# A Fourier mixing and ReGLU kernel: order of loads, products and tables in its set-up

## The chip, the cores and the metric

The kernel runs on one core of one Trainium2 chip. Its time is the device time of one execution in microseconds (us), smaller is better. An engine here is one of PE (TensorE, matrix products; PEld is its weight load), DVE (VectorE), ACT (ScalarE), POOL (GpSimd) and SP (SyncE, which here only issues transfers). Each engine works through its own list of instructions in order, and waits on semaphores for what others make. Transfers are issued from SP, ACT and POOL and run on 16 shared DMA engines.

## The reference

The input x has 8 batches of 3008 rows of 256 channels in float32. Each batch goes through a Fourier transform over its rows and one over its channels, of which the real part is kept; then follows a gated feed-forward layer with 1536 hidden units.

```python
X = np.fft.fft(x, axis=1)
X = np.fft.fft(X, axis=2)
y = X.real.astype(np.float32).reshape(8 * 3008, 256)
gate = np.maximum(y @ w_gate, 0.0)
val = y @ w_val
out = (gate * val @ w_out).astype(np.float32)
```

## The kernel before

The real part of the two transforms is U·C − V·S in effect: U and V are transforms of x over its rows with cosines and with sines, and the transform over the channels is folded into the weights. TA and TB (128 x 2 x 128, bf16) are the cosine and sine tables over the channels; WA = TA·w and WB = TB·w are the folded weights, for gate (index 0) and value (index 1). The row transform uses the symmetry of cosine and sine: a row and its mirror row are added first (XD holds rows of x, XG holds the mirror rows, AA their sums; F and G are what goes into the products), and tables tabC and tabS hold cosine and sine for six groups of 128 rows (c = 0 to 5). Row groups are handled in three tiles, t = 0, 1, 2, each with two halves r = 0, 1 (and a parity). Each half of a tile of XD or XG holds 256 KB.

All batches but the first are prepared while the matmuls of an earlier batch run. The first one can't be: before the main loop can start, the kernel has to load batch 0, make all tables and the folded weights, and do a first part of the row transform (the function dft_first, from L605). This is the set-up, the first 18.6 us of the profile. The order of work on each engine is written out by hand there; no scheduler moves it. After it the PE runs two products and a mirrored one for each of 12 blocks of hidden units (first_tile), with the second half of the folded weights (weights, L419, products L427) between them, and from the ninth block on also the output products (L782), which need the matrix wo.

The steps of the set-up that the change and the prediction touch:

- Loads of batch 0. The upper mirror rows of tile 0 (XG, L126) and rows of tile 0 (XD, L113) go out on SP and ACT, then rows of tile 1 on SP (L96). The rows of tile 2 are loaded by `load_rows(0, (2,))` (L96) with `load_last(0)` (L102) behind it; these stand on SP and wait for two writes to the same tile: `hold` (L116), a one-element memset on POOL whose only use is that the load has to wait for it, and a memset of the last 32 partitions on DVE (L381).
- Mirror rows of tiles 1 and 2: four indirect gathers on POOL (L120, load_mirror), (t, r) = (1,0), (1,1), (2,0), (2,1), called M10, M11, M20, M21 below. Between them stand small iota instructions (L274) that fill urow, from which the PE makes the angles; urow has one pair of rows for each pair of c.
- Behind the gathers POOL loads the weights (L342): first the 512 columns that dft_first needs (called w00 for gate, w10 for value), later four more such blocks, and wo (L417).
- turn(r) (L395) on PE puts the mirror rows of half r of tile 0 in the right order, by a float32 product with a reversed identity matrix. angle(n, c) makes the tables of one c: two products on PE (L360, L361), then three steps on ACT (L364 sine, L365 absolute value, L366 cosine). spin(n) issues n products on zeros (L326).
- On DVE, for each tile: sums AA (L472 and L473 for a half of tile 0, L461 and L462 for tiles 1 and 2), F (L441, L439), the middle channel hy (L447), G (L455). ACT then makes the small vector ny from hy (whole_128, L451).
- In dft_first: products(t, 0, ..) multiply F with tabC and products(t, 1, ..) multiply G with tabS (both L622); nyquist(t) multiplies ny with tabC (L628); combine(i) makes the first 512 columns of WA and WB (L636), gate first.
- The second halves of TA and TB are the first halves with signs changed on odd columns (L655, L656 on ACT). Column 0 of both is written by POOL (L349, L409).

Before the change the order on PE is: turn(0), the angles of c = 3, turn(1), the angles of c = 2, then in dft_first the products of tile 0 with the angles of c = 5 and 4 between them, tile 1, combine(0), tile 2, combine(1).

Of the kernel before, what the change touches and what calls it, by code (L numbers as in the profile page):

```python
# [15 lines left out]
ALU = mybir.AluOpType  # L16
# [13 lines left out]
def dram(ap, offset, pattern):  # L30
    return bass.AP(ap.tensor, offset, [list(p) for p in pattern])
# [3 lines left out]
def kernel(  # L35
# [8 lines left out]
    nc = tc.nc  # L44
    B, S, D = x.shape
    DF = moe_w_gate.shape[1]
    NF = DF // 128
    H = S // 2
# [14 lines left out]
    def single(name, shape, dt=F32, pool=const):  # L63
        return pool.tile(shape, dt, name=name, tag=name)
# [3 lines left out]
    WA = [single(f"WA{i}", [128, DF], BF16) for i in range(2)]  # L68
# [9 lines left out]
    XD = single("XD", [128, 2, 3, 2, D])  # L78
# [14 lines left out]
    def load_rows(b, ts=range(3)):  # L93
        for t in ts:
            n = (128, 128, 112)[t]
            nc.sync.dma_start(out=XD[0:n, :, t].rearrange("p r a d -> p r (a d)"),  # L96
                              in_=dram(x, (b * S + 1 + t * 256) * D, [[2 * D, n], [H * D, 2], [1, 2 * D]]))

    def load_last(b):
        for a in range(2):  # L100
            n = (8, 7)[a]
            nc.sync.dma_start(out=XD[112:112 + n, :, 2, a, :], in_=dram(x, (b * S + 1 + 2 * (256 + 112) + a) * D, [[2 * D, n], [H * D, 2], [1, D]]))  # L102
# [12 lines left out]
    def hold(ts):  # L115
        nc.gpsimd.memset(XD[0:1, :, ts, 0, 0:1], 0.0)  # L116

    def load_mirror(b, t, r):
        n = (128, 128, 120)[t]
        nc.gpsimd.indirect_dma_start(  # L120
            out=XG[0:n, r, t, :, :].rearrange("p a d -> p (a d)"), out_offset=None, in_=pairs,
            in_offset=bass.IndirectOffsetOnAxis(ap=gidx[0:n, 2 * t + r:2 * t + r + 1], axis=0), element_offset=b * S * D)
# [144 lines left out]
    for r in range(2):  # L267
        load_half(0, r, (nc.sync, nc.scalar)[r])
    load_rows(0, (1,))
    load_mirror_0(0)  # L270
    load_spare()

    def iota(dst, pattern, base, mult):
        nc.gpsimd.iota(dst, pattern=pattern, base=base, channel_multiplier=mult, allow_small_or_imprecise_dtypes=True)  # L274
# [21 lines left out]
    def scale(N):  # L296
        return 2.0 * PI / N * (1.0 - 1e-6)

    KA, UC, KC = 95, 256.0, 128.0
    urow = single("urow", [KA, 6, 128], F16, pool=st_)  # L300
# [6 lines left out]
    TA = single("TA", [128, 2, 128], BF16)  # L307
    TB = single("TB", [128, 2, 128], BF16)
    md = single("md", [128, 129], pool=st_)
    ad = single("ad", [128, 129], pool=st_)  # L310
# [11 lines left out]
    def spin(n):  # L322
        if n:
            p = psO.tile([128, 512], F32, name="o", tag="o")
        for _ in range(n):
            nc.tensor.matmul(p[:], lhsT=warm[:, 0:128], rhs=warm[:], start=True, stop=True)  # L326
# [7 lines left out]
    iota(back[:], [[0, 1]], 127, -1)  # L334
    iota(gidx[:].rearrange("p (t r) -> p t r", r=2), [[-128, 3], [-H // 2, 2]], H - 1, -1)
    load_mirror(0, 1, 0)
    iota(urow[0:1, 2:4], [[1, 2], [2, 128]], 257, 0)
    load_mirror(0, 1, 1)
    hold(slice(2, 3))

    def load_w(i, c):
        nc.gpsimd.dma_start(out=wr[i][c], in_=(moe_w_gate, moe_w_val)[i][:, c * 512:(c + 1) * 512].rearrange("(c p) f -> p c f", p=128))  # L342
    for r in range(2):
        load_mirror(0, 2, r)
    iota(urow[0:1, 4:6], [[1, 2], [2, 128]], 513, 0)
    nc.gpsimd.memset(urow[0:1, 5, 120:121], 0.0)
    load_w(0, 0)
    load_w(1, 0)
    nc.gpsimd.memset(TA[:, 0, 0:1], 0.5)  # L349

    nc.vector.tensor_scalar(us[:], u[:], scalar1=1.0 / S, op0=ALU.mult, scalar2=None)
    nc.scalar.activation(ums[:], half_pi[:], ACTF.Sin)
# [4 lines left out]
    def angle(n, c):  # L357
        home, tag = ((psG, "g"), (psD, "d"))[n % 2]
        m = home.tile([128, 512], F32, name=tag, tag=tag)
        nc.tensor.matmul(m[:, 0:NJ], lhsT=urow[:, c, :], rhs=krow[:], start=True, stop=False)  # L360
        nc.tensor.matmul(m[:, 0:NJ], lhsT=minus[:], rhs=quot[c][:], start=False, stop=True)  # L361
        r = slice(0, ROWS[c % 2][c // 2])
        act = nc.scalar.activation
        steps = [lambda: act(tabS[r, c, odd_k], m[r, 0:NJ], ACTF.Sin, scale=scale(S)),  # L364
                 lambda: act(mag[c][:], m[:, 0:NJ], ACTF.Abs),  # L365
                 lambda: act(tabC[r, c, odd_k], mag[c][r], ACTF.Sin, scale=-scale(S), bias=half_pi[r])]  # L366
        for step in steps if c != 4 else steps[1:] + steps[:1]:
            step()
# [10 lines left out]
    quotient(5)  # L379
    quotient(4)  # L380
    nc.vector.memset(XD[96:128, :, 2, 1, :], 0.0)  # L381
    load_rows(0, (2,))
    load_last(0)
    nc.vector.tensor_scalar(ums[:], pidx[:], scalar1=1.0 / D, op0=ALU.mult, scalar2=None)
    nc.vector.tensor_scalar(qd[:], dvec[:], scalar1=ums[:], op0=ALU.mult, scalar2=ROUND, op1=ALU.add)
# [7 lines left out]
    def turn(r):  # L393
        p = psV.tile([128, 512], F32, name="v", tag="v")
        nc.tensor.matmul(p[:], lhsT=turned[:], rhs=XG[:, r, 0, :, :].rearrange("p a d -> p (a d)"), start=True, stop=True)  # L395
        upright.append(p[:].rearrange("p (a d) -> p a d", a=2))

    spin(3)
    angle(0, 1)
    angle(1, 0)  # L400
    turn(0)
    nc.scalar.activation(ad[:], md[:], ACTF.Abs)
    nc.scalar.activation(TA[:, 0, 1:128], ad[:, 1:128], ACTF.Sin, scale=-scale(D), bias=half_pi[:])
    nc.scalar.activation(TB[:, 0, 1:128], md[:, 1:128], ACTF.Sin, scale=-scale(D))
    angle(2, 3)
    turn(1)
    angle(3, 2)

    nc.gpsimd.tensor_scalar(TB[:, 0, 0:1], ad[:, 128:129], scalar1=-1.0 / 128, op0=ALU.mult, scalar2=0.5, op1=ALU.add)  # L409
    iota(kvec[:, 0:NE], [[2, NE]], 0, 0)  # L410
    nc.gpsimd.memset(sg[:], 2.0)
    for i in range(2):
# [36 lines left out]
    def whole_128(t):  # L449
        p = slice(0, ROWS[1][t])  # L450
        nc.scalar.mul(ny[p, t], hy[p, t], 2.0)  # L451
# [5 lines left out]
    for t in range(3):  # L457
        n = ROWS[1][t]
        p = slice(0, n)
# [153 lines left out]
    def dft_first(U, V):  # L613

        raw, ends = [], [family(0, dst, 1, False, now=False, pool=pool) for dst, pool in ((U, (psP, "p")), (V, (psO, "o")))]
        bank = {(k, par): ends[k][2](par) for k in range(2) for par in (1, 0)}

        def products(t, k, rs):
            src, tab = ((FF[1], tabC), (GG[1], tabS))[k]
            for r, par in [(r, par) for r in rs for par in (1, 0)]:  # L620
                rows = slice(0, ROWS[par][t])
                nc.tensor.matmul(bank[k, par][:, 0:NJ], lhsT=src[rows, r, t, par, 0:128], rhs=tab[rows, 2 * t + par, odd_k],  # L622
                                 start=(t == 0 and r == 0), stop=(t == 2 and r == 1), skip_group_check=bool(k))

        def nyquist(t):
            for par in (1, 0):
                rows = slice(0, ROWS[par][t])
                nc.tensor.matmul(bank[1, par][0:1, 0:NJ], lhsT=ny[rows, t, par:par + 1], rhs=tabC[rows, 2 * t + par, odd_k],  # L628
                                 start=False, stop=False, skip_group_check=True)

        def combine(i, js):
            for j in js:
                home, tag = ((psV, "v"), (psV, "v"), (psG, "g"), (psD, "d"))[len(raw)]
                p = home.tile([128, 512], F32, name=tag, tag=tag)
                for kc in range(2):
                    nc.tensor.matmul(p[:], lhsT=(TA, TB)[j][:, kc, :], rhs=wr[i][0][:, kc, :], start=(kc == 0), stop=(kc == 1))  # L636
                raw.append(p)

        def whole(W, p):
            return W[:, 0:512], p[:]  # L640

        def by_vector(W, p):
            nc.vector.tensor_scalar(*whole(W, p), scalar1=1.0, op0=ALU.mult, scalar2=None)

        products(0, 0, (0,))
        products(0, 1, (0,))
        whole_128(0)
        angle(4, 5)
        products(0, 0, (1,))
        products(0, 1, (1,))  # L650
        nyquist(0)
        angle(5, 4)
        whole_128(1)
        for T in (TA, TB):
            nc.scalar.copy(T[:, 1, 0::2], T[:, 0, 0::2])  # L655
            nc.scalar.mul(T[:, 1, 1::2], T[:, 0, 1::2], -1.0)  # L656
        products(1, 0, (0, 1))
        nyquist(1)
        products(1, 1, (0, 1))
        combine(0, (0, 1))  # L660
        whole_128(2)
        nc.scalar.copy(*whole(WA[0], raw[0]))
        products(2, 0, (0, 1))
        ends[0][1](1)
        ends[0][1](0)
        evict.pop(0)()
        nc.vector.tensor_scalar(m2[:], pidx[:], scalar1=1.0, op0=ALU.min, scalar2=-2.0, op1=ALU.mult)
        sums[0]()
        by_vector(WB[0], raw[1])
        nyquist(2)  # L670
        products(2, 1, (0, 1))
        ends[1][1](1)
        ends[1][1](0)
        evict.pop(0)()
        sums[2]()
        combine(1, (0, 1))
        nc.scalar.copy(*whole(WA[1], raw[2]))
        nc.scalar.copy(*whole(WB[1], raw[3]))  # L678
        for k in (1, 3):
            sums[k]()  # L680
        del sums[:]
# [138 lines left out]
    EVEN_AT = (8, 10, 12, 14, 16, 17)  # L820
    CB = U
    dft_first(U, V)
    fold_even()
    turns_and_rows()
# [458 lines left out]
```

## Time and profile before

| what | us |
|---|---|
| median of 3 runs | 628.52 |
| lowest and highest run | 628.43, 628.83 |
| the profiled execution, its own time | 628.41 |
| its span from first to last instruction | 626.4 |
| busy PE / DVE / POOL / ACT | 618.8 / 547.7 / 523.4 / 455.6 |
| idle time of PE in the span | 7.6 |

In rows of the profile a line has start and duration in us, the engine, the source line (L), the operation, the tile it writes and those it reads, and in square brackets the idle time before it with what ended it. "x2" stands for two instructions merged in one row. Matmuls overlap, so that their ends in the timeline run past the start of the next one; the chain of waits shows each with the share of time that it alone takes. In rows of a transfer, the last number is the time in us from the start of its issue to its landing. In rows of a queue stand its packets, its MB, and the time of these packets as a share of 16 engines over the stretch asked for; q1 holds the transfers of SP, q10 those of ACT, q0 those of POOL.

### The profile page before, as it was taken

What the parts mean: (1) busy time and instruction counts of PE and PEld (TensorE: products, weight loads), DVE (VectorE), ACT (ScalarE), POOL (GpSimd) and SP (SyncE); (2) the same over time, 40 slices, a digit from 0 to 9 for tenths busy, and PEclk for the clock granted to TensorE, in tenths of its full rate; (3) what the DMA queues carried; (4) which work ended last, traced back from release to release, by engine and by line L of the source; (5) the groups of instructions that cost most, each with busy time, mean ns of one, the idle gap of its engine ahead of it and who ended that gap; (6) DMA issues with size and microseconds to landing.
All of it is one profiled execution on the core that took longest, in us unless ns stands there. A gap on an engine that the chain in (4) does not pass through costs nothing.

```text
span 626.4 us, 12435 instructions
## 1 busy us (share of the span) xinstructions
PE 618.8 (99%) x4095; PEld 397.7 (63%) x4095; DVE 547.7 (87%) x975; ACT 455.6 (73%) x837; POOL 523.4 (84%) x494
## 2 busy tenths in 40 slices
PE   8999999999999999999999999999999999999997
PEld 2566666666666666666666666666666666666666
DVE  8886676999899899988999899899999989999991
ACT  7796667767678777777777777777777768888872
POOL 8988992898899988799979989799896657898890
PEclk9999999999999999999999999999999999999999
DMA  9955758734364427315362426211211111211113
GB/s 240 211 201 133 167 179 101 190 72 145 86 150 143 127 75 190 109 44 166 82 189 64 141 77 125 59 54 48 77 53 45 43 60 38 61 51 45 58 43 103
DMA packets 86034, 66.48 MB, mean 106 GB/s; under 512 B 41639, under 2 KB 69063, under 8 KB 85970
## 3 DMA queue, kind: packets, MB, share of 16 engines
q1 hardware_dynamic: 81384, 60.02, 35.3%
q0 software_dynamic: 3984, 4.92, 3.9%
q8 instruction: 32, 0.52, 0.4%
q10 hardware_dynamic: 602, 0.75, 0.3%
q14 instruction: 32, 0.26, 0.1%
HBM read 41.89 MB, written 34.17 MB: 121 GB/s over the span
## 4 chain that ended last, share of the span: by engine, by line
PE 93%; DVE 3%; ACT 1%; issue 1%; DMA 1%; DVEq 0%; ACTq 0%
PE o L782 37%; PE v L880 10%; PE v L875 9%; PE v L874 9%; PE g L1021 8%; PE p L1028 8%; PE d L586 4%; DVE h L910 2%; PE p L880 1%; PE p L874 1%; PE p L875 1%; PE v L395 1%; DMA XG<-in_x_dram 1%; DVE h L899 1%; DVE r L1032 1%
## 5 line engine op out<-in xcount | busy, mean ns | idle before, releaser
L1033 POOL TENSOR_TENSOR r<-r 128x512 f32<-128x512 f32 (+1 forms) x247 | 308.0, 1254 | 77.7 <-DVE r L1032 76.3
L910 DVE SCALAR_TENSOR_TENSOR h<-r,v 128x512 bf16<-128x512 f32 (+1 forms) x486 | 307.8, 673 | 40.6 <-PE v L880 30.0
L782 PE MATMUL o<-wo,h 128*128 128x256 bf16 x2172 | 330.0, 272 | 0.0
L782 PEld LDWEIGHTS <-h 128*128 128x128 bf16 x2220 | 216.7, 98 | 111.7 <-issue 1.3
L1016 ACT ACTIVATE p<-CB,b 128x512 f32<-128x512 bf16 (+1 forms) x251 | 171.8, 685 | 66.9 <-DVE r L1032 65.2
L1024 ACT COPY r<-g 128x512 f32<-128x512 f32 (+1 forms) x247 | 142.6, 577 | 58.3 <-PE g L1021 49.3
L1032 DVE SCALAR_TENSOR_TENSOR r<-r,p 128x512 f32<-128x512 f32 (+1 forms) x247 | 165.2, 669 | 0.6 <-ACT r L1024 0.6
L875 PE MATMUL v<-V,WB 128*128 128x512 bf16 (+3 forms) x288 | 105.6, 367 | 0.0
L874 PE MATMUL v<-U,WA 128*128 128x512 bf16 (+3 forms) x288 | 105.6, 367 | 0.0
L1028 PE MATMUL p<-U,WA 128*128 128x512 bf16 (+1 forms) x251 | 94.1, 375 | 0.0
L1021 PE MATMUL g<-V,WM 128*128 128x512 bf16 (+1 forms) x247 | 92.6, 375 | 0.2
L880 PE MATMUL v<-V,WM 128*128 128x512 bf16 (+1 forms) x244 | 91.4, 375 | 0.7 <-DVE h L910 0.4
L899 DVE TENSOR_TENSOR h<-r,v 128x376 bf16<-128x376 f32 (+2 forms) x90 | 46.0, 545 | 17.6 <-PE v L880 8.9
L874 PEld LDWEIGHTS <-WA 128*128 128x128 bf16 x340 | 33.1, 97 | 38.8 <-issue 11.3
L795 ACT COPY os<-o 128x512 f32<-128x512 f32 x92 | 52.6, 571 | 3.4 <-PE o L782 3.4
L875 PEld LDWEIGHTS <-WB 128*128 128x128 bf16 x340 | 33.2, 98 | 32.7 <-ACT WB L678 0.2
L198 POOL TENSOR_TENSOR XG<-XG,XD 128x510 f32<-128x510 f32 x42 | 53.0, 1272 | 0.6 <-DMA XG<-xr 0.6
L890 ACT ACTIVATE r<-p 128x376 f32<-128x376 f32 (+1 forms) x80 | 38.0, 486 | 17.8 <-PE p L880 9.6
L206 POOL TENSOR_TENSOR AA<-XG 128x510 f32<-128x510 f32 x42 | 45.5, 1096 | 0.0
L1021 PEld LDWEIGHTS <-WM 128*128 128x128 bf16 x247 | 24.2, 98 | 5.6 <-issue 0.3
L1028 PEld LDWEIGHTS <-WA 128*128 128x128 bf16 x251 | 24.6, 98 | 3.3 <-issue 0.2
L880 PEld LDWEIGHTS <-WM 128*128 128x128 bf16 x245 | 24.0, 98 | 3.8
(201 smaller groups left out, 475.2 us busy)
## 6 DMA issues: line engine op xcount, KB each, us to landing
out_dram<-os SPq DMA_DIRECT2D x124, 128.0 KB
xr<-in_x_dram SPq DMA_DIRECT2D x12, 768.0 KB
XG<-xr SPq DMA_DIRECT2D x12, 768.0 KB
XD<-in_x_dram SPq DMA_DIRECT2D x15, 512.0 KB
out_dram<-os SPq DMA_DIRECT2D x35, 112.0 KB
XD<-in_x_dram SPq DMA_DIRECT2D x8, 448.0 KB
CB<-ch SPq DMA_DIRECT2D x7, 376.2 KB
out_dram<-os SPq DMA_DIRECT2D x13, 96.0 KB
```

What stands on the lines that cost most here:

```text
L198: e.tensor_tensor(XG[p, r, t, ::-1, 1:D], XG[p, r, t, ::-1, 1:D], XD[p, r, t, :, D - 1:0:-1], op=ALU.add)
L782: nc.tensor.matmul(st["p"][0:m, q, :], lhsT=lhs(f), rhs=wo[:, f, :], start=(f == 0 and not (early and q)), stop=(f == NF - 1), skip_group_ ...
L874: nc.tensor.matmul(bank[:, 0:st["n"]], lhsT=WA[i][:, st["f"]], rhs=st["us"], start=True, stop=False)
L875: nc.tensor.matmul(bank[:, 0:st["n"]], lhsT=WB[i][:, st["f"]], rhs=st["vs"], start=False, stop=True)
L880: nc.tensor.matmul(bank[:, 0:st["n"]], lhsT=W[i][:, st["f"]], rhs=v, start=False, stop=True, skip_group_check=True)
L910: nc.vector.scalar_tensor_tensor(half_h(st, sign), in0=st["s"][1 + sign][:, 0:n], scalar=0.0, in1=st["v"][:, 0:n], op0=ALU.max, op1=ALU.mult)
L1016: nc.scalar.activation(st["p"][:, 0:st["n"]], st["c"], ACTF.Copy, scale=b2[:, st["fi"]:st["fi"] + 1])
L1021: nc.tensor.matmul(st["g"][:, 0:n], lhsT=WM[0][:, st["f"]], rhs=st["vs"], start=True, stop=True)
L1024: nc.scalar.copy(q[:, 0:n], st["g"][:, 0:n])
L1028: nc.tensor.matmul(st["p"][:, 0:n], lhsT=WA[0][:, st["f"]], rhs=st["us"], start=False, stop=True, skip_group_check=True)
L1032: nc.vector.scalar_tensor_tensor(sp[:, 0:n], in0=q[:, 0:n], scalar=-0.5, in1=st["p"][:, 0:n], op0=ALU.mult, op1=ALU.add)
L1033: nc.gpsimd.tensor_tensor(sm[:, 0:n], sp[:, 0:n], q[:, 0:n], op=ALU.add)
```

## The change

Six things are moved or split, all of them in the set-up:

1. The rows of tile 2 come in two loads: `load_part(0, 96)` on SP behind a `hold` that now stands before the second gather (M11) and not behind it, and `load_part(96, 112)` where the whole load was.
2. The iota for urow c = 2, 3 moves behind the third gather.
3. One `spin` product is added, and turn(1) follows turn(0) directly, ahead of the angles of c = 3.
4. The second halves of TA and TB are made on ACT directly behind the first halves, not in dft_first; their column 0 is written by POOL together with that of the first halves.
5. In dft_first the PE does the angles of c = 4 ahead of nyquist(0), and nyquist(1) behind both products of tile 1.
6. ACT does whole_128(1) ahead of the tables of c = 4, and the copy of the first folded weights ahead of whole_128(2).

```diff
+    def load_part(p, q):
+        nc.sync.dma_start(out=XD[p:q, :, 2].rearrange("p r a d -> p r (a d)"), in_=dram(x, (513 + 2 * p) * D, [[2 * D, q - p], [H * D, 2], [1, 2 * D]]))
...
     load_mirror(0, 1, 0)
-    iota(urow[0:1, 2:4], [[1, 2], [2, 128]], 257, 0)
+    hold(slice(2, 3))
+    load_part(0, 96)
     load_mirror(0, 1, 1)
-    hold(slice(2, 3))
...
-    for r in range(2):
-        load_mirror(0, 2, r)
+    load_mirror(0, 2, 0)
+    iota(urow[0:1, 2:4], [[1, 2], [2, 128]], 257, 0)
+    load_mirror(0, 2, 1)
...
-    nc.gpsimd.memset(TA[:, 0, 0:1], 0.5)
+    nc.gpsimd.memset(TA[:, :, 0:1], 0.5)
...
-    load_rows(0, (2,))
+    load_part(96, 112)
     load_last(0)
...
     angle(1, 0)
+    spin(1)
     turn(0)
+    turn(1)
...
+    for T in (TA, TB):
+        nc.scalar.copy(T[:, 1, 2::2], T[:, 0, 2::2])
+        nc.scalar.mul(T[:, 1, 1::2], T[:, 0, 1::2], -1.0)
     angle(2, 3)
-    turn(1)
     angle(3, 2)
 
-    nc.gpsimd.tensor_scalar(TB[:, 0, 0:1], ad[:, 128:129], scalar1=-1.0 / 128, op0=ALU.mult, scalar2=0.5, op1=ALU.add)
+    nc.gpsimd.tensor_scalar(TB[:, :, 0], ad[:, 128:129].to_broadcast([128, 2]), scalar1=-1.0 / 128, op0=ALU.mult, scalar2=0.5, op1=ALU.add)
...
         products(0, 1, (1,))
+        whole_128(1)
+        angle(5, 4)
         nyquist(0)
-        angle(5, 4)
-        whole_128(1)
-        for T in (TA, TB):
-            nc.scalar.copy(T[:, 1, 0::2], T[:, 0, 0::2])
-            nc.scalar.mul(T[:, 1, 1::2], T[:, 0, 1::2], -1.0)
         products(1, 0, (0, 1))
+        products(1, 1, (0, 1))
         nyquist(1)
-        products(1, 1, (0, 1))
         combine(0, (0, 1))
+        nc.scalar.copy(*whole(WA[0], raw[0]))
         whole_128(2)
-        nc.scalar.copy(*whole(WA[0], raw[0]))
         products(2, 0, (0, 1))
```

## The prediction

> **What bounds the kernel now.** I read the chain of waits over the whole span first. It says that the PE sets the end:
>
> ```profile
> PE 93%; DVE 3%; ACT 1%; issue 1%; DMA 1%; DVEq 0%; ACTq 0%
> ```
>
> So what the set-up can bring is the time by which the PE's unbroken run of products starts sooner. The same chain, asked for the first 24 us, shows where that run starts:
>
> ```profile
> 4.53 2.05 PE v L395 x2
> 6.58 0.31 PE g L360
> 7.20 1.71 PE v L395 x2
> 8.91 0.23 PE d L360
> 9.33 0.49 ACT tabS L364
> 13.69 0.10 ACT ny L451
> 13.84 0.48 PE o L628 x2
> 14.31 0.74 PE o L622 x4
> 15.06 0.86 PE v L636 x4
> 15.94 0.83 PE p L622 x4
> 18.37 0.43 PE d L636 x2
> ```
>
> The PE makes turn(0), one angle, turn(1), the next angle; from 9.33 to 13.8 the ACT's tables are the chain; and nyquist(1) waits for ny, which stands behind all tables on ACT. From 13.84 the PE has no gap up to the main loop. Next I read the timeline of DVE, ACT and PE, since the chain shows one path alone:
>
> ```profile
> 8.95 0.69 DVE L472 TENSOR_TENSOR AA<-v,XD 128x510 f32<-128x510 f32 x1 [0.45 <-PE v L395]
> 10.62 1.22 DVE L461 TENSOR_TENSOR AA<-XG,XD 128x1020 f32<-128x1020 f32 x1
> 13.92 1.22 DVE L461 TENSOR_TENSOR AA<-XG,XD 121x1020 f32<-121x1020 f32 x1 [0.35 <-issue]
> 15.45 0.43 DVE L441 TENSOR_TENSOR F<-AA 121x258 bf16<-121x258 f32 x1
> 12.56 0.83 PE L622 MATMUL p<-tabC,F 128*128 128x376 bf16 x4 [0.47 <-DVE F L441]
> 13.69 0.25 ACT L655 COPY TA<-TA 128x64 bf16<-128x64 bf16 x1
> 14.11 0.28 ACT L656 ACTIVATE TB<-TB 128x64 bf16<-128x64 bf16 x1
> ```
>
> F of tile 2 is done at 15.45 + 0.43 = 15.88, and the products that read it begin at 15.94. DVE's tile 2 is therefore a second path of the same length, and whatever takes time out of PE and ACT alone gains nothing. What did tile 2 wait for at 13.92? The view of transfers, asked for the moment of each issue, answers:
>
> ```profile
> 4.99 0.99 POOL L120 DMA_INDIRECT XG<-in_x_dram,gidx  x1 [0.17 <-issue]
> XG<-in_x_dram,gidx POOLq DMA_INDIRECT x1, 5.0
> 7.60 0.97 POOL L120 DMA_INDIRECT XG<-in_x_dram,gidx  x1 [0.30 <-issue]
> XG<-in_x_dram,gidx POOLq DMA_INDIRECT x1, 6.2
> 6.10 0.32 SPq L96 DMA_DIRECT2D XD<-in_x_dram  x1
> ```
>
> M11 lands at 4.99 + 5.0 = 10.0 and M21 at 7.60 + 6.2 = 13.8. That is 0.1 ahead of tile 2's start, so M21 sets it. The rows of tile 2 that SP issues at 6.10 are through q1 by 11, well ahead of M21. Loading them sooner helps only by leaving the DMA engines to M20 and M21 later.
>
> **The change part by part.** *Turns in a row.* It is the same PE work in another order: turn(1) ends at 4.53 + 2.05 + 1.71 = 8.29, not 8.91. DVE is busy with the first half of tile 0 until 8.50 (8.95 less its idle 0.45), so the second half starts at about 8.48 and tile 1 could start at 10.15, 0.47 sooner. The price: the angle of c = 3 comes 1.7 later on PE, done at 8.91. ACT's tables of c = 3 start there, those of c = 2 follow (1.5 each, as 9.33 to 10.8), and the last of them ends near 11.9, 1.1 later than now. The added spin product (0.43) lies in the PE's wait for tile 0:
>
> ```profile
> 4.53 2.05 PE L395 MATMUL v<-XG,turned 128*128 128x512 f32 x2 [0.47 <-DMA XG<-in_x_dram]
> ```
>
> Without that cover it would cost its 0.43 on PE, of which DVE's 0.2 of reserve at 8.29 would hide half.
>
> *Table halves and ny.* Four small ACT steps, 13.69 to 14.39 = 0.7, move to about 7.7 to 8.4, where ACT now has to wait for the angles anyhow: free. ny of tile 1 no longer stands behind the tables of c = 4. ACT then runs: c = 2 to 11.9, ny of tile 0, c = 5 to 13.4, ny of tile 1 (its hy is there), c = 4 to 15.0. The cosine of c = 4, needed first, is there 0.4 ahead of that, at 14.6. The PE is through with nyquist(0) at 12.5, tile 1's two product groups at 14.1, nyquist(1) at 14.5, combine(0) at 15.36: 0.58 ahead of 15.94. Should the tables not be late, this bound falls away and DVE's is left: tile 1 at 10.15, tile 2 no sooner than 2.95 behind it (13.92 − 10.62 − 0.35), at 13.10 and not 13.92, 0.82 gained.
>
> *POOL's order.* The hold is one short memset, the iota costs 0.48:
>
> ```profile
> 4.34 0.48 POOL L274 IOTA urow<- 1x256 f16 x1
> ```
>
> Without the iota ahead of it M11 is issued at 4.6, M20 at 5.9, M21 at 7.5. The iota for c = 2, 3 ends near 7.35, and the PE wants it at 8.29; with that cover gone the angle waits as long as the iota is late. The one-column writes on POOL get a second column each: 0 to 0.05, nothing queued behind them before 12 is due. On SP only the 16-row rest and the last rows stand behind the new load, and they wait for the memset at 5.66 as before.
>
> *The load.* Its first 96 rows go out at 4.6 and not 6.10, right behind tile 1's rows, so that they meet M10 and M11 on the engines:
>
> ```profile
> q0 software_dynamic: 150, 0.52, 83.4%
> q1 hardware_dynamic: 102, 0.16, 21.1%
> q1 hardware_dynamic: 281, 0.48, 68.7%
> q1 hardware_dynamic: 614, 1.19, 71.7%
> q0 software_dynamic: 613, 0.31, 45.3%
> q0 software_dynamic: 203, 0.41, 99.4%
> q0 software_dynamic: 8, 0.00, 1.2%
> 3.04 1.28 POOL L120 DMA_INDIRECT XG<-in_x_dram,gidx  x1 [0.31 <-POOL gidx L274]
> 4.50:9.00 4.50, 4.47 (x8) 1.78 (x9) 3.70 (x14) 3.90 (x10) 3.74 (x6) 1.00 1.05 330
> ```
>
> The first two rows are 6.5 to 9.0 (M10 and M11, 0.52 MB), the third 8.5 to 11 (the load, 0.48 MB), the next two 22 to 27, where both queues have work and packet goes against packet, 614 to 613. The sixth is 11 to 13: gathers alone, 205 GB/s. The seventh is 9.0 to 9.5: M11's bytes are through by 9.0, 1.0 ahead of its landing. If the queues share like that, M10 and M11 are through after 150 packets of each side: 0.52 + 0.06 + 0.24 MB at the 330 GB/s of 4.5 to 9 is 2.5 us, at 9.0 as now; M11 cannot begin before some 8.0 and then shares, so I take 9.3, landing at 10.3 with the 1.0 that it takes now. Lower end: 9.6, from the issue 0.4 sooner. Upper end: rival A. Tile 1 then starts at 10.4. M20 and M21 have the engines to themselves from 9.3: 0.49 MB at 205 GB/s is 2.4, but M21, issued at 7.5, moves no sooner than 3.4 after its issue (M10 issued at 3.04, first packets of q0 at 6.5), so 10.9 + 1.2 = 12.1, landing 1.0 to 1.3 later, at 13.1 to 13.4 and not 13.8. Tile 2 starts at 10.4 + 2.95 = 13.35, its F is done at 15.3, the PE is there at 15.36. Gain at tile 2: 0.55.
>
> The Trainium skill, "DMA: Bandwidth & Descriptors", section "Queues, rings and completion order", says that each DMA engine takes turns between the queues that have work, a packet at a time. The counts of 22 to 27 agree; by that rule the sum is the one above. The stretch 9.0 to 9.5 looks unlike it, with q0 at 8 packets while the load moved, though M20 had been issued, and by that row the sum is rival A's.
> *What is late next.* Behind the gathers q0 carries the weights and wo without a gap:
>
> ```profile
> 9.04 0.81 POOL L342 DMA_DIRECT2D h<-in_moe_w_gate_dram  x1
> h<-in_moe_w_gate_dram POOLq DMA_DIRECT2D x1, 256.0 KB, 5.5
> 15.40 1.06 POOL L417 DMA_DIRECT2D wo<-in_moe_w_out_dram  x1
> wo<-in_moe_w_out_dram POOLq DMA_DIRECT2D x1, 768.0 KB, 14.9
> 30.35 0.49 PE L782 MATMUL o<-wo,h 128*128 128x256 bf16 x3
> ```
>
> w00 lands at 9.04 + 5.5 = 14.5, just as combine(0) comes to want it. wo lands at 15.40 + 14.9 = 30.3, and its first reader starts at 30.35: no reserve. A PE that comes 0.55 sooner, at 29.8, meets wo, which moves by what q0's stream moves: nothing at the least, 0.6 at the most (M21's bytes gone at 12.0 and not 12.5, and the issues behind them on time). I take 0.35, as M21 and the weights are issued 0.1 sooner and the stream can close up by most of the rest. Sum: 628.41 − 0.35 = 628.06 against the profiled execution's own time; that lies 0.11 below the median of the runs, so 628.2.
>
> **The rivals.** A, *the load holds the gathers up* (slower). If q0 gets little while q1 has work, the load takes 6.7 to 9.1 (its 2.4 now), and the rest of M10 and M11, 0.43 MB at 360 to 205 GB/s, ends at 10.3 to 11.2, landing at 11.3 to 12.2. Tile 1 starts 0.8 to 1.7 late, tile 2 at 14.35 to 15.25 and not 13.92: 0.4 to 1.3 lost, 628.9 to 629.8. It decides from a start of tile 1 later than 10.97. For it: the 8 packets. Against: 613 to 614. B, *it is hidden anyway*: M21 still lands at 13.8, or wo at 30.3; either ends the gain at 0.05 or less, 628.5. For it: M21 is issued only 0.1 sooner, and wo has no reserve. C, *everything closes up*: M11 by 10.1, the tables not late, wo 0.6 or more sooner; 0.6 to 0.82 gained, 627.7 to 627.9. Against: three conditions at once.
>
> **How the numbers follow.** Forecast 0.40, its own range 627.9 to 628.4; B 0.23; A 0.19; C 0.18. The time is the forecast's, 628.2. The range 627.5 to 629.1 leaves out the upper half of A (about 0.09) and what may lie beyond C. A measurement of this kernel tells about 0.2%, or 1.26 us, from no change. Only the far end of A reaches that: slower 0.08. DVE's order bounds C at 0.82; I leave 0.08 of C's chance to a larger gain, for small waits behind 30 us that may close up and which I have not followed. The rest, 0.84, is within 0.2%.
>
> **What would show it.** DVE's idle 0.45 ahead of the second half of tile 0 is gone (right for the turns); tile 1's L461 starts near 10.4 (after 10.97: A); M21 lands near 13.2 and tile 2's L461 starts at 13.35; the products of tile 2 start near 15.4; the first L782 starts near 30.0, with the landing of wo just ahead of it. A gap of the PE between nyquist(0) and combine(0) over 0.3 would show the late tables as the bound. The prediction fails if L782 starts later than 30.4 or sooner than 29.5, or if the difference at L782 is not the difference at the end.

## The result, and the profile after

| | before | after |
|---|---|---|
| median of the runs, us | 628.6 (6 runs, 628.43 to 628.83) | 630.91 (6 runs, 630.61 to 632.15) |
| ratio after to before, of the means | | 1.0041, 95% interval 1.0031 to 1.0052 |
| the profiled execution, us | 628.41 | 630.74 |
| its span, us | 626.4 | 628.6 |
| busy PE in the span, us | 618.8 | 619.8 |
| mean granted clock of the runs | 1.0 (the profiled one) | 0.997 in four runs, 0.995 in two |

The change makes the kernel 0.4% slower, about 2.3 us, where 0.3 us less was forecast. PE is busy 1.0 us longer though it computes the same (and one small product on zeros more): two things happened, not one. The chain's shares on the page of the changed kernel show little of it:

```profile
PE 93%; DVE 4%; issue 1%; DMA 1%; POOL 1%; ACT 1%; DVEq 0%; POOLq 0%; ACTq 0%
```

So again the chain of waits over the first 34 us, now of the changed kernel (start, us, what):

```profile
4.62 5.09 DMA XG<-in_x_dram,gidx
9.71 0.33 DVE G L463
10.04 2.17 issue
12.21 1.23 DVE AA L469
...
13.68 0.44 DVE F L449
14.12 0.05 issue
14.16 1.44 PE p L630 x4
15.60 1.25 PE o L630 x4
16.85 0.71 PE o L636 x2
17.57 0.97 PE v L644 x4
18.54 0.65 PE p L630 x4
...
32.92 0.33 PE o L787 x3
```

ACT's tables, which filled this chain from 9.33 to 13.8 before, are gone from it. In their place stands the gather M11, issued at 4.62, and a pause of 2.17 us, marked "issue", up to DVE's tile 1 at 12.21. Behind that, four products take 1.44 us that took 0.83 to 0.86 before. (The chain names no releaser for the pause and calls it "issue"; the landing of M11, below, shows what it was.) The timeline of the changed kernel has the same from the engines' side, DVE first, then PE:

```profile
8.30 0.68 DVE L480 TENSOR_TENSOR AA<-v,XD 128x510 f32<-128x510 f32 x1
12.21 1.22 DVE L469 TENSOR_TENSOR AA<-XG,XD 128x1020 f32<-128x1020 f32 x1 [2.17 <-issue]
15.10 1.21 DVE L469 TENSOR_TENSOR AA<-XG,XD 121x1020 f32<-121x1020 f32 x1
14.16 1.44 PE L630 MATMUL p<-tabC,F 128*128 128x376 bf16 x4 [2.53 <-DVE F L449]
15.39 1.46 PE L630 MATMUL o<-tabS,G 128*128 128x376 bf16 x4
32.76 0.49 PE L787 MATMUL o<-wo,h 128*128 128x256 bf16 x3
```

The second half of tile 0 starts at 8.30 with no idle before it, so the turns did what they were meant to. Tile 1 starts at 12.21, against 10.62. Tile 2 follows directly, at 15.10 against 13.92: it now waits for tile 1 and no longer for M21. PE stands for 2.53 us, and then runs at half speed. The output product starts at 32.76 against 30.35, 2.41 late, and the execution ends 2.33 late. What tile 1 waited for is in the transfers of the changed kernel, M11 and then M21, each with its issue and its time to landing:

```profile
4.62 1.12 POOL L123 DMA_INDIRECT XG<-in_x_dram,gidx  x1
XG<-in_x_dram,gidx POOLq DMA_INDIRECT x1, 7.5
7.58 0.99 POOL L123 DMA_INDIRECT XG<-in_x_dram,gidx  x1 [0.19 <-issue]
XG<-in_x_dram,gidx POOLq DMA_INDIRECT x1, 6.7
```

M11 lands at 4.62 + 7.5 = 12.1, 2.1 later than before although issued 0.4 sooner. M21 lands at 7.58 + 6.7 = 14.3. The queues of the changed kernel (packets, MB, share of the engines) show what moved meanwhile, the first two rows from 8 to 9, the others from 9 to 10:

```profile
q1 hardware_dynamic: 140, 0.28, 108.3%
q0 software_dynamic: 3, 0.00, 0.2%
q0 software_dynamic: 42, 0.17, 66.3%
q1 hardware_dynamic: 70, 0.11, 46.0%
```

For a whole microsecond the load has the engines and the gathers move next to nothing, 3 packets. The second effect is in the view of stretches of the changed kernel (busy us of PE, PEld, DVE, ACT and POOL with counts, then the granted clock):

```profile
10.62:14.03 3.41, 0.77 (x4) 0.09 (x2) 1.75 (x4) 1.83 (x5) 3.35 (x10) 1.00 1.07 202
14.03:17.44 3.41, 3.28 (x10) 1.08 (x10) 3.27 (x11) 1.56 (x4) 1.45 (x2) 0.50 1.24 204
17.32:20.70 3.38, 3.38 (x18) 1.47 (x18) 1.93 (x8) 1.64 (x4) 1.48 (x4) 0.98 1.24 204
```

From 14.03 to 17.44, just as tile 1's products come, the clock is granted at 0.50. In the 3.41 us ahead of that PE was busy for 0.77 us. In the kernel before it is 1.00 from 10.49 to 17.32, with PE busy for 5.90 of these 6.83 us.

### The profile page after: what moved, and what is told of

Read it like the earlier page. It is cut to its first block, busy times and chain, and to the rows that moved or that the text cites. A ratio compares the mean times of both kernels' runs of the same rounds, so it can differ in the third digit from the quotient of the medians.

```text
span 628.6 us, 12440 instructions
## 1 busy us (share of the span) xinstructions
PE 619.8 (99%) x4096; PEld 398.0 (63%) x4096; DVE 548.1 (87%) x975; ACT 455.5 (72%) x837; POOL 522.4 (83%) x494
## 4 chain that ended last, share of the span: by engine, by line
PE 93%; DVE 4%; issue 1%; DMA 1%; POOL 1%; ACT 1%; DVEq 0%; POOLq 0%; ACTq 0%
PE o L787 37%; PE v L885 10%; PE v L880 9%; PE v L879 9%; PE g L1026 8%; PE p L1033 8%; PE d L594 4%; DVE h L915 2%; PE p L885 1%; PE p L879 1%; PE p L880 1%; DMA XG<-in_x_dram,gidx 1%; DVE r L1037 1%; PE o L435 1%; DVE h L904 0%
```

## The experiments

The theory after the result: the sooner load holds M11 up (the wait, about 1.0 us at the end), and the PE's pause lets the clock fall (1.3 us more); the rest of the change by itself costs and brings nothing. The rival: one of the rearrangements on PE, ACT or POOL costs the time. All runs are set beside runs of the kernel before on the same chip.

**e1, the load at its old place, all else kept.**

```diff
     load_mirror(0, 1, 0)
-    hold(slice(2, 3))
-    load_part(0, 96)
     load_mirror(0, 1, 1)
+    hold(slice(2, 3))
...
-    load_part(96, 112)
+    load_rows(0, (2,))
```

> The changed kernel with the rows of tile 2 loaded in one piece where they were before, behind a hold that stands behind the second gather (M11); all other parts of the change stay. Theory S (the load sooner is what costs: it holds M11 up by some 2 us, and the PE's long wait then lets its clock fall): M11 lands at 9.7 to 10.1, tile 1 on DVE starts at 10.1 to 10.2, no stretch at half clock, the first output product at 29.9 to 30.3, and the time is 628.0 to 628.5, at or below the kernel before. Rival T (the new order of turns, angles, ny and table halves costs by itself): tile 1 early as well, but the PE waits between nyquist(0) and the products of tile 2 for tables, and the time stays over 629.5.

Measured: 628.66 (11 runs, 628.21 to 628.95) against 628.7; ratio 0.9998 (0.9989 to 1.0007). The timeline of e1:

```profile
10.50 1.22 DVE L468 TENSOR_TENSOR AA<-XG,XD 128x1020 f32<-128x1020 f32 x1 [0.47 <-issue]
14.04 1.22 DVE L468 TENSOR_TENSOR AA<-XG,XD 121x1020 f32<-121x1020 f32 x1 [0.57 <-issue]
12.45 0.83 PE L629 MATMUL p<-tabC,F 128*128 128x376 bf16 x4 [0.82 <-DVE F L448]
```

The whole loss is gone, so there is none without the sooner load; the rival falls. The other five parts of the change are together worth nothing that these runs can tell: tile 1 starts 0.12 sooner than before, tile 2 waits 0.57 us for M21 all the same and starts at 14.04.

**e2, the load alone: the kernel before with the sooner load.**

```diff
+    def load_part(p, q):
...
     iota(urow[0:1, 2:4], [[1, 2], [2, 128]], 257, 0)
+    hold(slice(2, 3))
+    load_part(0, 96)
     load_mirror(0, 1, 1)
-    hold(slice(2, 3))
...
-    load_rows(0, (2,))
+    load_part(96, 112)
```

> The kernel before with the split and sooner load alone. Theory S: M11 (issued behind the iota as before, at 5.0) lands near 12, tile 1 starts at 12.0 to 12.4 and not 10.62, and the time is 630 to 631. Whether the clock falls here tells what set it off: in the old order PE has other products in the gap, so the half-clock stretch may be missing, and then the time is near 630.0. Rival T: below 629.

Measured: 628.95 (10 runs, 628.62 to 630.08), ratio 1.0005 (0.9996 to 1.0014). The timeline of e2, whose profiled execution was its longest run (630.08):

```profile
11.46 1.22 DVE L465 TENSOR_TENSOR AA<-XG,XD 128x1020 f32<-128x1020 f32 x1 [1.17 <-issue]
13.41 0.83 PE L626 MATMUL p<-tabC,F 128*128 128x376 bf16 x4 [1.74 <-DVE F L445]
14.59 1.22 PE L626 MATMUL o<-tabS,G 128*128 128x376 bf16 x4
```

The load alone does not bring the loss: the interval has 1 in it. Tile 1 is late in this profile, but by 0.84 and not 1.6, and the clock fell in this one of the ten runs (its next products take 1.22 and not 0.83; granted clock 0.997, 0.999 to 1.0 in the others). Here the iota still stands ahead of the load, which goes out at 5.10 and not 4.63, and the two queues shared: from 8 to 9 the load moved 72 packets and the gathers 48, where it was 140 to 3, and M11 landed at 5.03 + 6.4 = 11.4. So the loss needs the sooner load together with another part of the change. That this is the iota, with its 0.47, was not tried by itself.

**e3 and e8, the pause filled.** The changed kernel with 14 (e3, shown) or 6 (e8) products more behind nyquist(0); nothing reads their result.

```diff
         nyquist(0)
+        again = psV.tile([128, 512], F32, name="v", tag="v")
+        for _ in range(14):
+            nc.tensor.matmul(again[:, 0:NJ], lhsT=FF[1][:, 0, 0, 1, 0:128], rhs=tabC[:, 1, odd_k], start=True, stop=True)
         products(1, 0, (0, 1))
```

> The changed kernel with 14 repeated products (128x376, into a spare bank, their result is not used) behind nyquist(0), where the PE otherwise waits 2.5 us for tile 1. Theory: the wait itself costs 1.6 and the fall of the clock behind it 1.0; with the gap filled the granted clock stays whole, tile 1's and tile 0's products take 0.83 and 0.75 and not 1.44 and 1.25, M11 still lands near 12.1, and the time is 629.6 to 630.0, 0.9 to 1.2 below the changed kernel. Rival (the products of tile 1 are slow for another reason, such as DVE giving G late, and the clock costs nothing): within 0.3 of the changed kernel, 630.6 to 631.

> The changed kernel with 6 repeated products behind nyquist(0), not 14: about 1.0 of the 2.5 us of the wait is filled. If the clock falls where a stretch of some 3.4 us holds too little PE work, wherever that stretch happens to begin, then runs spread between two values: near 629.6, as with 14 products, where it does not fall, and 630.5 to 631 where it does. If it is the whole wait that counts, all runs lie at 629.5 to 629.9.

Measured: e3 629.65 (11 runs, 629.37 to 630.13), ratio 1.0015 (1.0006 to 1.0024). e8 629.58 (11 runs, of which ten 629.25 to 629.64 and one 631.2), ratio 1.0017 (1.0008 to 1.0026). The timeline of e3:

```profile
12.50 1.22 DVE L469 TENSOR_TENSOR AA<-XG,XD 128x1020 f32<-128x1020 f32 x1 [2.46 <-issue]
11.56 2.40 PE L664 MATMUL v<-tabC,F 128*128 128x376 bf16 x14
14.45 0.84 PE L630 MATMUL p<-tabC,F 128*128 128x376 bf16 x4 [0.48 <-DVE F L449]
17.39 0.83 PE L630 MATMUL p<-tabC,F 121*128 121x376 bf16 x4
```

and that of e8:

```profile
11.56 1.13 PE L664 MATMUL v<-tabC,F 128*128 128x376 bf16 x6
14.35 0.83 PE L630 MATMUL p<-tabC,F 128*128 128x376 bf16 x4 [1.66 <-DVE F L449]
```

Tile 1 is as late as ever (12.50, even 0.29 later than in the changed kernel's profile), yet its products run in 0.84 us. This splits the loss, each beside the kernel before on its own chip: with the pause filled 629.65 − 628.7 = 0.95 us are left of 2.31, so the wait is worth about 1.0 us and the clock the other 1.36. e8 gives 629.58 − 628.55 = 1.03 for the wait; its one run at 631.2 has a granted clock of 0.997, the others 0.999 to 1.0, so the runs fall into the two groups that were expected. The profile agrees: from tile 1's first products to tile 2's it takes 17.39 − 14.45 = 2.94 us here and 18.54 − 14.16 = 4.38 in the changed kernel, 1.44 more.

**e4, a third of the load sooner.** `load_part(0, 32)` early, `load_part(32, 112)` at the old place.

```diff
-    load_part(0, 96)
+    load_part(0, 32)
...
-    load_part(96, 112)
+    load_part(32, 112)
```

> The changed kernel with 32 rows of tile 2 loaded sooner, not 96, and 80 rows at the later place. If the gather waits for the bytes of the load that are ahead of it, a third of the dose gives a third of the delay: M11 lands at 10.4 to 10.9 and the time is 628.4 to 629.2. If any transfer that is issued between the gathers throws M11 back by a fixed time, M11 lands near 12 as with 96 rows. If it is the 80 rows, issued at about 5.7, that meet M11 as well, it lands between, 11 to 12.

Measured: 628.82 (10 runs, 628.45 to 630.28), ratio 1.0006 (0.9996 to 1.0015). The timeline of e4:

```profile
10.77 1.22 DVE L469 TENSOR_TENSOR AA<-XG,XD 128x1020 f32<-128x1020 f32 x1 [0.73 <-issue]
14.13 1.22 DVE L469 TENSOR_TENSOR AA<-XG,XD 121x1020 f32<-121x1020 f32 x1 [0.39 <-issue]
```

M11 lands at 4.62 + 6.1 = 10.7, in the range expected if the bytes of the load count. 32 rows hold tile 1 up by 0.27 against e1, 96 rows by 1.71: more bytes, more delay, though a third of them gives less than a third of it.

**e5 and e7, the load behind the gathers.** If the load in front costs, it may gain behind: `hold` behind M21 (e5; the load goes out at 8.69) or behind M20 (e7; at 7.13), the load whole, the rest of the change kept. The edit is that of e5:

```diff
     load_mirror(0, 1, 0)
-    hold(slice(2, 3))
-    load_part(0, 96)
     load_mirror(0, 1, 1)
...
     load_mirror(0, 2, 1)
+    hold(slice(2, 3))
...
-    load_part(96, 112)
+    load_rows(0, (2,))
```

> The first experiment's kernel with the hold, and so the load of tile 2's rows, behind the last gather (M21); the load then goes out near 8.7. Theory: a gather's first packets wait until the load on the other queue has drained, so with the load last all gathers land sooner, M11 near 10.0, M20 at 11.0 to 11.6, M21 at 12.2 to 12.8, and tile 2 then waits for its own rows, which land near 13.2 to 13.8: 628.2 to 628.6, at best 0.4 below the kernel before. Rival (the gathers are slow by themselves, each some 3 us from the end of its issue to its first packet): M20 lands near 13 as before, the load comes on top, tile 2 starts at 14.2 or later, 628.8 to 629.3.

> The first experiment's kernel with the hold behind the third gather (M20), the load going out near 7.1. Theory (gathers wait for a load ahead of them to drain): M20 lands at 11.0 to 11.6 and M21, now behind the load, at 13.8 to 14.1: 628.5 to 628.8. Rival (slow gathers): M20 near 13, M21 near 14, the same time. Only the landing of M20 tells them apart here.

Measured: e5 628.74 (11 runs, 628.41 to 630.53), ratio 1.0004 (0.9995 to 1.0013); e7 628.67 (11 runs, 628.23 to 628.93), ratio 1.0002 (0.9993 to 1.0011). The timeline of e5, with M21's time to landing in the last row:

```profile
9.95 1.22 DVE L468 TENSOR_TENSOR AA<-XG,XD 128x1020 f32<-128x1020 f32 x1
14.14 1.22 DVE L468 TENSOR_TENSOR AA<-XG,XD 121x1020 f32<-121x1020 f32 x1 [1.24 <-DMA XD<-in_x_dram]
15.22 0.59 PE L643 MATMUL v<-h,TA 128*128 128x512 bf16 x2 [1.36 <-DMA h<-in_moe_w_gate_dram]
XG<-in_x_dram,gidx POOLq DMA_INDIRECT x1, 4.1
```

and of e7, in the same way:

```profile
9.99 1.22 DVE L468 TENSOR_TENSOR AA<-XG,XD 128x1020 f32<-128x1020 f32 x1
14.07 1.22 DVE L468 TENSOR_TENSOR AA<-XG,XD 121x1020 f32<-121x1020 f32 x1 [1.13 <-DMA XG<-in_x_dram,gidx]
XG<-in_x_dram,gidx POOLq DMA_INDIRECT x1, 6.4
```

With no load ahead of it M21 takes 4.1 us and lands at 11.7; with the load ahead 6.4, at 14.0. So it was the load that made M21 late in the kernel before too. M20, which was to tell the readings of e7 apart, lands there at 6.03 + 4.8 = 10.8 and not near 13: the gathers are not slow by themselves. Tile 1 is 0.67 sooner than before in e5. But tile 2 waits as before: in e5 for its own rows, in e7 for M21, to 14.1 in both. The kernel before, e1, e4, e5, e6 and e7 bring tile 2's data in different orders, and it is complete between 13.8 and 14.1 each time.

**e6, the load on two queues.** As e1, but one half r on SP and the other on ACT.

```diff
...
-    load_part(96, 112)
+    def load_side(r, queue):
...
+    load_side(0, nc.sync)
     load_last(0)
...
     angle(1, 0)
+    load_side(1, nc.scalar)
     spin(1)
```

> The first experiment's kernel with the load of tile 2's rows split in its two halves, one from SP, one from ACT (at about 6.4, where ACT waits for DVE). Theory: one queue alone moves the load at 280 GB/s, the two of the start moved 400, so the load is through 0.6 sooner, M20 starts sooner and M21 lands at 13.3 to 13.6 and not 13.96; tile 2 starts 0.4 to 0.6 sooner, and the time is 628.1 to 628.5. Rival (M20 does not wait for the load, or the engines are full either way): M21 lands at 13.8 to 14.1 and the time is that of the first experiment, 628.66.

Measured: 628.38 (11 runs, 628.25 to 629.96), ratio 1.0001 (0.9992 to 1.001). Tile 1 starts at 10.51, tile 2 at 13.96. No gain: a second queue did not bring the data of tile 2 sooner.

**e9, tile 1 without gathers.** As e6, but the mirror rows of tile 1 come in two plain loads in upward order and PE turns them like tile 0's; M10 and M11 are dropped.

```diff
+    for r in range(2):
+        load_upward(1, r, (nc.sync, nc.scalar)[r])
     load_rows(0, (1,))
...
-    load_mirror(0, 1, 0)
     hold(slice(2, 3))
-    load_part(0, 96)
-    load_mirror(0, 1, 1)
...
+            if t:
+                turn(0, 1)
+                turn(1, 1)
...
```

> A version that tries to beat both: the experiment with two queues, and besides the mirror rows of tile 1 come as two plain loads (one from SP, one from ACT) and are turned on PE like those of tile 0, in place of the gathers M10 and M11. Theory (tile 2 waits for the last of all bytes, and gathers move 205 GB/s where two plain queues move 400): two gathers fewer are 0.5 MB at twice the speed, some 1.2 us of the engines' time, so M21 lands at 12.7 to 13.2; DVE, which now handles tile 1 in halves, bounds tile 2 at 13.3 to 13.5 and not 13.92, and the time is 627.9 to 628.3. Rival (the engines are no faster for it, or the turns of tile 1 hold the PE up): tile 2 starts at 13.9 or later, 628.5 or more.

Measured: 629.58 (11 runs, 629.3 to 630.0), ratio 1.0016 (1.0006 to 1.0025): slower. The timeline of e9:

```profile
7.59 0.34 ACTq L386 DMA_DIRECT2D XD<-in_x_dram  x1
7.97 0.31 ACT L411 ACTIVATE ad<-md 128x129 f32<-128x129 f32 x1 [1.54 <-DVE AA L488]
14.43 1.22 DVE L472 TENSOR_TENSOR AA<-XG,XD 121x1020 f32<-121x1020 f32 x1 [0.94 <-DMA XD<-in_x_dram]
```

ACT's half of the load is issued only at 7.59 (5.99 in e6); ACT stands idle for 1.54 us around it, and tile 2's rows land 6.53 after the issue, at 14.1. What the issue waited for was not found out. DVE is through with tile 1 at 13.5, as expected, so this says little of the idea: one load came too late. Tile 2's start, 0.51 later than before, is only about half of the loss of 0.95; the rest was not followed. No version run here beats the kernel before by more than its interval.

**e10, the changed kernel again**, later, beside 15 runs of the kernel before on the same chip.

> The changed kernel itself once more, on the same chip as the other: 630.5 to 631.2 in most runs, with one half-clock stretch, a few runs near 632 with two; any run without such a stretch should lie near 629.6, where the filled gaps put it.

Measured: 631.14 (5 runs, 630.84 to 632.13), ratio 1.0038 (1.0024 to 1.0052). Granted clock 0.997 in four runs and 0.995 in the fifth, the longest. The loss and the clock's fall are the changed kernel's own.

## Why the prediction was wrong

- *The bound.* Right as far as it went: PE's run, fed by two paths of the same length, one of them tile 2 on DVE behind M21.
- *Turns in a row, the table halves, ny, the spin product.* Right. The second half of tile 0 started at 8.30 (forecast 8.48), and DVE was free for tile 1 at 10.04 (10.15). The two turns took 3.40 us together and not 3.76 and ended at 4.27 + 3.40 = 7.67, not 8.29, but DVE was not free sooner. The feared late tables did not bind: the only pause on PE between nyquist(0) and combine(0) was released by DVE's F, not by ACT. e1, in which all this is kept, shows no cost and no gain.
- *POOL's order.* Right: M11 issued at 4.62, M20 at 6.04, M21 at 7.58 (forecast 4.6, 5.9, 7.5).
- *The load: the step that failed.* "If the queues share like that, M10 and M11 are through after 150 packets of each side", and from it "I take 9.3, landing at 10.3". It landed at 12.1. The packet counts of 22 to 27 us, 614 to 613, were taken as the rule for this place; the row that was at hand from the place itself, 9.0 to 9.5 with 8 packets of q0, was put down as the lesser evidence. From 8 to 9 the changed kernel moved 140 packets of the load and 3 of the gathers. This is rival A as it was worked out: landing 11.3 to 12.2, tile 1 0.8 to 1.7 late (it was 1.59), tile 2 at 14.35 to 15.25 (15.10). Its mechanism had 0.19 and was the right one.
- *The rule of the Trainium skill.* "DMA: Bandwidth & Descriptors", section "Queues, rings and completion order", has the engines take turns packet by packet. The 140 to 3 packets of 8 to 9 do not fit an even exchange, and the measurement decides; whether all of M11's packets were ready by then no view shows. In e2, 72 to 48 in the same microsecond, the two queues did share.
- *Tile 2's gain of 0.55.* It rested on M20 and M21 having the engines to themselves from 9.3. e5 shows what they do when they really have (M21 lands at 11.7), and that it brings nothing: the load then comes last, and tile 2 starts at 14.14. The data of tile 2 was complete at 13.8 to 14.1 in every order of e1 and e4 to e7, so the 0.55 was not to be had by any of these orders. The forecast looked at M21 by itself, not at the last of the transfers that tile 2 needs.
- *What was not in the sum at all: the clock.* The prediction asked what a late tile 1 costs DVE, never what a pause of PE costs PE. Rival A was priced at "0.4 to 1.3 lost, 628.9 to 629.8". e3 and e8, in which the pause is filled, measured just that, 629.65 and 629.58. The other 1.3 to 1.4 us are the half clock. So the mechanism of rival A was right and its price was not: it lacked this term.
- *wo without reserve.* Not put to the test: the changed kernel's PE comes 2.41 us later to wo, which lands at 14.41 + 16.2 = 30.6.
- *"If the difference at L782 is not the difference at the end."* Nearly the same: 2.41 and 2.33. The other sign held: that product started at 32.76, later than 30.4.

The sum as it should have been, from the profiles: tile 2 on DVE 15.10 − 13.92 = 1.18 late, the products of tile 1 and combine(0) 1.44 longer at half clock, 2.62 together; tile 2's products start 18.54 − 15.94 = 2.60 late, of which 2.3 is left at the end.

## What to carry to other kernels

When a transfer is moved forward, list all transfers that the same consumer needs and ask which lands last: with the engines full, another order only changes which one it is, while what was first and is now behind the moved one is late at once. Price contention with a row of the same kinds of transfers at the same place; what was one to one elsewhere in this kernel was 140 to 3 here, and 72 to 48 in e2, with the load issued 0.47 us later. And a pause on TensorE has two prices, its own length and the clock afterwards, so look up the granted clock behind every pause that a change may open, also one that the rest of the pipeline would make good.

## What the runs showed of the hardware

**A plain load on SP's queue can shut out POOL's queue for about a microsecond, and need not.** Packets in the microsecond in which the load moves the most bytes:

| kernel | stretch, us | load's queue (q1) | POOL's queue (q0) |
|---|---|---|---|
| changed | 8 to 9 | 140 | 3 |
| changed, again (e10) | 8 to 9 | 131 | 11 |
| before | 9 to 10 | 134 | 8 |
| e1 | 9 to 10 | 129 | 11 |
| e7 | 10 to 11 | 124 | 2 |
| e5 | 11 to 12 | 126 | 0 |
| e2 | 9 to 10 | 101 | 42 |
| e4 | 9 to 10 | 89 | 48 |

In the first five rows a gather had been issued and moved next to nothing (0.03 MB at most); in e5 the four gathers are in by 11.7, and the weights wait: PE stands 1.36 us for w00 at 15.22. In e2 and e4 both queues move. What decides between the two, and why the queues alternate from 22 to 27 us, stays open.

**The clock can fall for 3.41 us after a pause of PE that is shorter than that.** In the changed kernel, with pauses of 2.53 and 2.97 us in two profiles, the granted clock was 0.997 or less in 11 of 11 runs; one half-clock stretch of 3.41 us is 3.41 · 0.5 / 628 = 0.0027 of the mean. For the other kernels stands the longest pause from 10 us on in their one profile. In e3, whose pause is 0.48 us, it fell in 0 of 11; in e8, with six products ahead of 1.66 us, in 1 of 11; in e2 (1.74 us) in 1 of 10; in e4 (1.07 us) in 2 of 10; in e5 (1.36 us) and e6 (0.83 us) in 1 of 11 each; in e1 (0.82 us), e7 (0.97 us) and e9 (0.78 us) in none. The first two runs with 0.995 took 632.11 and 632.15, against 630.61 to 631.08 of the four others: 1 to 1.5 us for a second stretch. The profile of the third, in e10, shows it: the clock is 0.50 from 13.05 to 19.87, twice 3.41 us on end. The Trainium skill, "TensorE: Matmul & The Clock Gate", section "Part 1: The HAM clock gate (the "warmup" mystery)", has a free-running window of 3413 ns and half rate after an idle one. The length agrees with the 3.41 us, and a window that runs free would fit the falls that come in some runs only; but PE was busy for 0.77 us in the 3.41 ahead of the fall, so it need not be idle throughout. In the two other profiles with a fall it was busy for even more of these 3.41 us: 1.70 in e10 (9.64 to 13.05) and 1.68 in e2 (11.44 to 14.85). In the kernel before, whose 81 runs beside the experiments all have a granted clock of 0.999 or 1.0, it was busy for 2.50 from 10.49 to 13.90. Where the line lies was not measured.

**A small POOL write beside a large sum on DVE.** In the timeline of before the write of one column of TB stands beside DVE's tile 1 (10.62 to 11.84):

```profile
10.66 1.21 POOL L409 TENSOR_SCALAR TB<-ad 128x1 bf16<-128x1 f32 x1
```

and in that of the changed kernel, with two columns, it starts at the same moment while DVE is idle:

```profile
10.66 0.23 POOL L417 TENSOR_SCALAR TB<-ad 128x2 bf16<-128x2 f32 x1
```

Five times longer beside the sum, and done when the sum is. It is not the number of columns: the write of two columns took 1.12 us beside the sum in e1. Nothing hung on it here. The Trainium skill, "SBUF — State Buffer", section "Who interferes with whom", says that a DVE instruction with two inputs in SBUF holds up a GpSimd instruction that reads SBUF; these two rows agree.
